# The last expert's second layer with seven block products in place of the plain product, and the stores around it

## The chip, the cores and the metric

The kernel runs on one core of a Trainium2 chip. The metric is the time of one execution on the device in microseconds (us); the runs shown are given by their median. One execution more was taken with the hardware profiler; its trace is what is read here.

## The reference

```python
def _attn_ref(q, k, v):                     # q, k, v: (8, 8, 576, 64)
    k_p = k.reshape(B, H, Sp, 8, D).mean(axis=3)      # keys and values pooled by 8
    v_p = v.reshape(B, H, Sp, 8, D).mean(axis=3)
    scores = scale * np.matmul(q, k_p.transpose(0, 1, 3, 2))
    attn = softmax(scores)
    return np.matmul(attn, v_p)

def _moe_ref(x, domain_probs, w1, w2):      # x: (4608, 512), w1: (4, 512, 1024), w2: (4, 1024, 512)
    p = domain_probs / (domain_probs.sum(-1, keepdims=True) + 1e-09)
    for e in range(E):
        h = np.maximum(x @ w1[e], 0.0)
        out += p[:, e:e + 1] * (h @ w2[e])
    return out
```

The output of the attention, with the heads side by side, is the x of the second part. Four experts each do two layers on all 4608 rows.

## The kernel before

The rows are worked through in nine chunks of 512. Chunks 0 to 7 are the first 512 rows of each batch, chunk 8 holds the remaining 64 of all batches. For each chunk the attention's result lies transposed in `xT`; then the four experts follow. Matmuls are in bf16, sums are kept in f32.

**Block products.** Both layers cut their operands into 2 x 2 blocks and form the product from seven block products in place of eight, with sums of blocks that are made beforehand and afterwards (Winograd's form of Strassen's scheme). For the second layer of expert `e`, `quarters` names the four blocks of the hidden layer H: `a11`, `a12`, `a21`, `a22` (first index: the two row halves of 256 rows, second: the two halves of the 1024 hidden columns). `hidden_sums` makes four sums of them on VectorE: part 0 is S3 = a11 - a21, part 1 is S2 = a22 - S3, part 2 puts a21 + a22 in the place of a21, part 3 puts a12 - S2 in the place of a12. The sums of the weights lie in `wt_bf`, and `w2_bf`'s block b12 is overwritten with b12 - b22. One block product has 2 row blocks of 128 (index `j`) x 4 slices of the hidden columns: 8 matmuls of 128 x 256.

**The order.** Instructions stand in each engine's queue in the order of the program text (a manual schedule). The main loop runs over `g`. At each `g` there are one block product for each of two halves of the first layer (`up_product`, steps 0 to 6, in PSUM banks `units[0]` and `units[1]`, one `g` apart) and one block product of the second layer of the expert before (`down`, steps 0 to 6, in two banks `chains`). `up_product` ends with a copy or a relu on ScalarE (steps 0 to 5 but 4) or a relu with an added part on VectorE (`relu_sum`, steps 4 and 6). `down` ends with two adds into `acc` on VectorE (`add`, line 842: the product by the row's probability plus `acc`); step 4 goes by ScalarE into `addend` and from there by GpSimd into `acc` (lines 775 and 777).

**The end.** With 32 pairs of chunk and expert in `order`, the last `g` is 224. There, the first layer's last product (unit 1, step 6) of chunk 8, expert 3 and step 6 of `down` for expert 2 are issued. Then `down_last` does expert 3's second layer as a plain product: for each of the four output quarters (row half `row`, column half `col`) two row blocks x 8 slices, 64 matmuls in all (line 822), each quarter with two adds. For it, block b12 of the weights, which was overwritten, is loaded again (`load_last_weights`, a DMA on GpSimd's queue). PSUM banks: the two row blocks of a quarter share one, except in the last quarter.

**Stores.** `store` writes a quarter of `acc` to the output. Up to chunk 7 it is one DMA on SP's queue (line 852). For chunk 8 it is two (line 856), one of 64 partitions on SP's queue and one of the other 64 on ScalarE's. In `down_last` three quarters are stored whole (128 KB on each queue), and the last one as two row blocks (64 KB on each queue for each). The kernel's closing stands under line 1122 in the trace: SP waits there for everything that is under way.

Of the kernel before, what the change touches and what calls it, by code (L numbers as in the profile page):

```python
# [9 lines left out]
ACT = mybir.ActivationFunctionType  # L10
ALU = mybir.AluOpType
# [6 lines left out]
def kernel(  # L18
# [10 lines left out]
    nc = tc.nc  # L29

    B, H, S, D = q.shape
    E, DM, F = moe_w1.shape
    P = nc.NUM_PARTITIONS
# [4 lines left out]
    NR = NT // P  # L38
    REM = S - NT
    KC = DM // P  # L40
    FCH = F // P
# [15 lines left out]
    HF, HN, HD, HK = FCH // 2, NT // 2, DM // 2, KC // 2  # L57
    FH = F // 2
    LO, HI = slice(0, HF), slice(HF, FCH)
    BLOCKS = 2  # L60
# [5 lines left out]
    units = [None, None]  # L66
    chains = [psum.tile([P, NT], F32, name=f"o_ps{i}") for i in range(2)]
# [6 lines left out]
    w2_bf = wpool.tile([P, E, FCH, DM], BF16, name="w2_bf")  # L74
    wu_bf = wpool.tile([P, E, 3, HK, FH], BF16, name="wu_bf")
    wt_bf = wpool.tile([P, E, 3, HF, HD], BF16, name="wt_bf")
    acc = const.tile([P, NR, DM], F32, name="acc")
    x_rem = const.tile([P, NPAIR, NT], BF16, name="x_rem")
    ident = const.tile([P, P], BF16, name="ident")
    partial = const.tile([P, 2, 2, NT], F32, name="partial")  # L80
    addend = const.tile([P, BLOCKS, HD], F32, name="addend")
    S2 = const.tile([P, HF, HN], BF16, name="S2")
    S3 = const.tile([P, HF, HN], BF16, name="S3")
# [24 lines left out]
    def choose_rows():  # L108
        nc.vector.memset(begun, 1.0)
        nc.gpsimd.affine_select(  # L110
            out=begun, in_=begun, compare_op=ALU.is_ge, fill=0.0, base=0,
            pattern=[[1, ROWS], [-POOL, SP + 1]], channel_multiplier=ROWS,
        )

    def rows_chosen(half):
        combine(takes[half * PR:(half + 1) * PR], begun[:, :, 0:SP], ALU.subtract, begun[:, :, 1:])
# [104 lines left out]
    p_all = const.tile([P, NBLK, E], F32, name="p_all")  # L221
# [23 lines left out]
    def combine(dst, a, op, b):  # L245
        nc.vector.tensor_tensor(out=dst, in0=a, in1=b, op=op)  # L246
# [352 lines left out]
    hidden = {(0, 0): H_bufs[0], (0, 1): H_bufs[1], (0, 2): H_third, (0, 3): H_bufs[0]}  # L599
    order = [(c, e) for c in range(1, NCH) for e in range(E)]  # L600
# [130 lines left out]
    def quarters(c, e):  # L731
        H_sb = hidden[(c, e)]
        return H_sb[:, 0, 0], H_sb[:, 1, 0], H_sb[:, 0, 1], H_sb[:, 1, 1]

    def hidden_sums(c, e, part):
        a11, a12, a21, a22 = quarters(c, e)
        if part == 0:
            combine(S3[:], a11, ALU.subtract, a21)
        elif part == 1:
            combine(S2[:], a22, ALU.subtract, S3[:])  # L740
        elif part == 2:
            combine(a21, a21, ALU.add, a22)
        else:
            combine(a12, a12, ALU.subtract, S2[:])
# [48 lines left out]
        if fcs.stop == FCH:  # L793
            add(o_ps, c, e, r, slice(0, DM), True)

    room = wu_bf[:, 0, 0].rearrange("p k (i d) -> p (k i) d", d=HD)

    def load_last_weights():

        nc.gpsimd.dma_start(  # L800
            out=room, in_=moe_w2[E - 1][0:FH, HD:DM].rearrange("(fc p) d -> p fc d", p=P)
        )

    def last_weights(fc, col):
        if col and fc < HF:
            return room[:, fc, :]
        return w2_bf[:, E - 1, fc, col * HD:(col + 1) * HD]

    def down_last(c, e):

        H_sb = hidden[(c, e)]
        banks = units[0] + units[1]
        for row in (1, 0):
            for col in range(2):
                cols = slice(col * HD, (col + 1) * HD)
                both = [banks[2 * row + col]] * BLOCKS
                if not row and col:
                    both[1] = chains[0]
                ps = [ps[:, j * HD:(j + 1) * HD] for j, ps in enumerate(both)]
                for j in range(BLOCKS):  # L820
                    for fc in range(FCH):
                        nc.tensor.matmul(  # L822
                            ps[j], lhsT=H_sb[:, fc // HF, row, fc % HF, j * P:(j + 1) * P],
                            rhs=last_weights(fc, col),
                            start=(fc == 0 and (j == 0 or both[1] is not both[0])),
                            stop=(fc == FCH - 1), skip_group_check=True,
                        )
                for j in range(BLOCKS):
                    add(ps[j], c, e, row * BLOCKS + j, cols, False)
                    if not row and col:  # L830
                        store(c, row, cols, j)
                if row or not col:
                    store(c, row, cols)

    def add(o_ps, c, e, r, cols, first):

        prob = p_all[:, c * NR + r, e:e + 1]
        dst = acc[:, r, cols]
        if e == 0 and first:
            nc.scalar.activation(out=dst, in_=o_ps, func=ACT.Copy, scale=prob)  # L840
        else:
            nc.vector.scalar_tensor_tensor(  # L842
                out=dst, in0=o_ps, scalar=prob, in1=dst, op0=ALU.mult, op1=ALU.add,
            )

    def store(c, row, cols, j=None):
        rs = slice(row * BLOCKS, (row + 1) * BLOCKS)
        if j is not None:
            rs = slice(rs.start + j, rs.start + j + 1)
        if c < B:  # L850
            rows = out[c * S:c * S + NT, :].rearrange("(p r) d -> p r d", r=NR)
            nc.sync.dma_start(out=rows[:, rs, cols], in_=acc[:, rs, cols])
        else:
            by_batch = out.rearrange("(b s) d -> s b d", s=S)[NT:S]
            for bb, queue in enumerate((nc.sync, nc.scalar)):
                queue.dma_start(
                    out=by_batch[:, 2 * rs.start + bb:2 * rs.stop:2, cols],
                    in_=acc[bb * REM:(bb + 1) * REM, rs, cols],
                )
# [172 lines left out]
    with tc.manual_schedule(  # L1032
            engines={ENG.PE, ENG.DVE, ENG.Activation, ENG.Pool, ENG.SP}):
        load_q(0)
        load_first(k, "kraw", 0)
        load_first(k, "kraw", 1)
        choose_rows()
        make_identity(nc, ident[:])
        load_first(v, "vraw", 0)
        load_first(v, "vraw", 1)  # L1040
        nc.gpsimd.memset(p_all[:], 0.0)
        load_probs()
        load_w1(0)
        load_w1(1)
        clear()
        rows_chosen(0)
        rows_chosen(1)
        load_w1(2)
        load_w2(0)
        load_w1(3)  # L1050
        attention_first()
        psum_first.__exit__(None, None, None)
        psum_last = ctx.enter_context(
            tc.tile_pool(name="psum_last", bufs=1, space=bass.MemoryType.PSUM))
        units[:] = [[psum_last.tile([P, NT], F32, name=f"unit{u}{i}") for i in range(2)] for u in range(2)]
        load_whole(1, k, "kraw")
        load_q(1)
        load_w2(1)
        load_whole(1, v, "vraw", 2)
        load_w2(2)  # L1060
        first_chunk()


        N = len(order)
        later, amid = pieces_later()
        below_of = [(0, 3)] + order
        sums = {}
        for at, pieces in (((3,), weight_sums(3)[3:]), ((10, 10, 11, 11), weight_sums(1)), ((10, 15, 22, 14), weight_sums(2))):
            for slot, piece in zip(at, pieces, strict=True):
                sums.setdefault(slot, []).append(piece)  # L1070
        POOLED = (4,)
        for g in range(7 * N + 1):
            t, i = divmod(g, 7)
            if i in (0, 2, 3) and 1 < g < 7 * N:
                hidden_sums(*below_of[t], i)
            t2, i2 = divmod(g - 1, 7)
            ups = [(*order[t], 0, i)] if t < N else []
            if 0 <= t2 < N:
                ups.append((*order[t2], 1, i2))

            for args in reversed(ups) if g in amid else ups:
                up_product(*args)
            if g in amid:
                amid[g]()
            if i == 1 and 1 < g < 7 * N:
                hidden_sums(*below_of[t], i)
            if g == 0:

                down_plain(0, 2, NR - 1)
            else:  # L1090
                down(*below_of[t2], i2, t2 % 2, POOLED)
            for piece in later.get(g, ()):
                piece()
            for piece in sums.get(g, ()):
                piece()
            if g == 7 * (N - 2):
                load_last_weights()
        down_last(*order[-1])
# [1 line left out]
_INS = ['q', 'k', 'v', 'moe_domain_probs', 'moe_w1', 'moe_w2']  # L1100
_OUTS = [((4608, 512), 'float32')]
# [25 lines left out]
```

## Time and profile before

| what | us |
|---|---|
| median of 3 runs (lowest, highest) | 489.6 (489.58, 489.82) |
| profiled execution, whole time | 489.93 |
| its span, first to last instruction | 488.2 |
| TensorE busy (share of the span) | 480.5 (98%) |
| VectorE busy | 376.9 (77%) |
| ScalarE busy | 303.8 (62%) |
| GpSimd busy | 119.4 (24%) |
| the plain product of `down_last` on TensorE, 64 matmuls | 476.9 to 483.9 |
| the last add on VectorE | 484.0 to 484.4 |

Times in the profile count from the first instruction. The mean granted clock of TensorE is 0.999. A busy time is the sum of an engine's instructions; instructions on one engine can overlap (a matmul takes 0.27 us from start to end, and the next starts 0.11 us after it), so what an instruction costs its queue is read from start to start.

### The profile page before, as it was taken

To read this page: it belongs to the slowest core of one execution; us is meant where nothing else is said; L and a number is where in the kernel's file an instruction comes from. 1 tells how busy PE (TensorE), PEld (TensorE's weight loads), DVE (VectorE), ACT (ScalarE), POOL (GpSimd) and SP (SyncE) were. 2 spreads that over 40 slices of the span, in tenths; PEclk is the share of its full clock that TensorE was granted. 3 is DMA by queue.
4 is the path that set the end of the run, shared out by engine and by line. 5 is a ranking of instruction groups with operands and counts; after the bars stand their busy time and mean duration, and the time that the engine had idled before them with its cause. 6 is when DMAs were issued, how large, how long until landed. Compare 5 with 4: busy or idle time off the path is not lost.

```text
span 488.2 us, 11522 instructions
## 1 busy us (share of the span) xinstructions
PE 480.5 (98%) x4673; PEld 409.4 (84%) x4678; DVE 376.9 (77%) x758; ACT 303.8 (62%) x576; POOL 119.4 (24%) x120
## 2 busy tenths in 40 slices
PE   8999999999999999999999999999999999999996
PEld 4669568898888888888888888888898888888885
DVE  4779799989768976798679866997678766876674
ACT  5677446855676567656765567556755567556650
POOL 8520504242523154016321442111011101010000
PEclk9999999999999999999999999999999999999999
DMA  9999999994986489345954298311111010004003
GB/s 195 203 209 203 204 170 155 103 90 54 110 110 63 77 86 137 35 83 56 159 50 91 27 165 66 68 23 66 35 23 23 23 64 3 12 23 87 1 1 87
DMA packets 104996, 41.96 MB, mean 86 GB/s; under 512 B 75504, under 2 KB 104432, under 8 KB 104944
## 3 DMA queue, kind: packets, MB, share of 16 engines
q0 software_dynamic: 58496, 22.35, 41.8%
q1 hardware_dynamic: 45328, 17.84, 16.7%
q10 hardware_dynamic: 1120, 1.05, 0.6%
q8 instruction: 36, 0.59, 0.5%
q14 instruction: 16, 0.13, 0.1%
HBM read 45.69 MB, written 9.44 MB: 113 GB/s over the span
## 4 chain that ended last, share of the span: by engine, by line
PE 91%; DMA 3%; ACT 2%; DVE 2%; POOL 1%; issue 1%; POOLq 0%; ACTq 0%
PE unit L695 42%; PE o_ps L763 41%; DMA w_bf<-in_moe_w_dram 3%; PE att L467 1%; PE unit L822 1%; PE o_ps L617 1%; PE att L393 1%; ACT expT L549 1%; PE unit L617 1%; PE unit L393 0%; DVE wt_bf L246 0%; POOL wt_bf L142 0%; ACT qT L378 0%; DVE acc L842 0%; PE work_first L631 0%
## 5 line engine op out<-in xcount | busy, mean ns | idle before, releaser
L842 DVE SCALAR_TENSOR_TENSOR acc<-o_ps,p_all,acc 128x256 f32<-128x256 f32 (+1 forms) x285 | 126.9, 485 | 52.9 <-PE o_ps L763 36.5
L763 PEld LDWEIGHTS <-H 128*128 128x128 bf16 x1320 | 129.1, 98 | 15.5 <-issue 0.6
L695 PEld LDWEIGHTS <-w_bf 128*128 128x128 bf16 x1088 | 105.2, 98 | 13.0 <-issue 0.2
L675 DVE CUSTOM_DVE_ANT_0 H<-unit,partial 128x512 bf16<-128x512 f32 x128 | 87.2, 684 | 23.8 <-ACT partial L710 11.5
L763 PE MATMUL o_ps<-w_bf,H 128*128 128x256 bf16 x792 | 102.6, 273 | 0.4 <-ACT o_ps L771 0.4
L695 PE MATMUL unit<-xT,w_bf 128*128 128x256 bf16 x704 | 100.5, 273 | 0.0
L777 POOL TENSOR_TENSOR acc<-acc,addend 128x512 f32<-128x512 f32 x24 | 30.7, 1279 | 253.2 <-ACT addend L775 202.2
L710 ACT COPY partial<-unit 128x512 f32<-128x512 f32 x128 | 72.3, 592 | 30.2 <-PE unit L695 30.2
L695 PEld LDWEIGHTS <-wu_bf 128*128 128x128 bf16 x816 | 77.6, 98 | 11.7 <-issue 2.5
L695 PE MATMUL unit<-xs,wu_bf 128*128 128x256 bf16 x512 | 77.0, 273 | 0.0
L763 PE MATMUL o_ps<-wt_bf,H 128*128 128x256 bf16 x528 | 68.4, 273 | 0.0
L712 ACT ACTIVATE H<-unit 128x512 bf16<-128x512 f32 x66 | 39.8, 605 | 30.9 <-PE unit L695 30.9
L763 PEld LDWEIGHTS <-S 128*128 128x128 bf16 x528 | 51.7, 98 | 6.0
L716 ACT ACTIVATE H<-unit 128x512 bf16<-128x512 f32 x66 | 39.6, 602 | 25.6 <-PE unit L695 25.3
L708 ACT COPY unit<-unit 128x512 f32<-128x512 f32 x68 | 39.4, 582 | 23.6 <-PE unit L695 18.0
L695 PE MATMUL unit<-xs,w_bf 128*128 128x256 bf16 x256 | 38.4, 273 | 0.0
L840 ACT ACTIVATE acc<-o_ps,p_all 128x256 f32<-128x256 f32 x72 | 30.7, 485 | 9.4 <-PE o_ps L763 7.7
L152 POOL DMA_DIRECT2D kraw<-in_k_dram x20 | 26.3, 1317 | 39.0 <-DMA kraw<-in_k_dram 39.0
L695 PE MATMUL unit<-xT,wu_bf 128*128 128x256 bf16 x240 | 35.7, 272 | 0.0
L763 PE MATMUL o_ps<-w_bf,S 128*128 128x256 bf16 x264 | 34.2, 273 | 0.0
L763 PE MATMUL o_ps<-wt_bf,S 128*128 128x256 bf16 x264 | 34.2, 273 | 0.0
L152 POOL DMA_DIRECT2D vraw<-in_v_dram x20 | 28.4, 1420 | 18.8 <-DMA vraw<-in_v_dram 18.5
(162 smaller groups left out, 500.2 us busy)
## 6 DMA issues: line engine op xcount, KB each, us to landing
out_dram<-acc SPq DMA_DIRECT2D x32, 256.0 KB, 4.2
w_bf<-in_moe_w_dram POOLq DMA_DIRECT2D x10, 512.0 KB, 17.4
q_sb<-in_q_dram POOLq DMA_DIRECT2D x7, 512.0 KB, 9.6
vraw<-in_v_dram POOLq DMA_DIRECT2D x22, 144.0 KB, 6.5
kraw<-in_k_dram POOLq DMA_DIRECT2D x21, 144.0 KB, 5.7
w_bf<-in_moe_w_dram POOLq DMA_DIRECT2D x2, 1024.0 KB, 17.8
w_bf<-in_moe_w_dram POOLq DMA_DIRECT2D x4, 256.0 KB, 7.3
wt_bf<-in_k_dram POOLq DMA_DIRECT2D x4, 144.0 KB, 5.4
```

Source lines behind the costliest of these rows:

```text
L152: nc.gpsimd.dma_start(out=raw[:], in_=rows_of(src, b, 2 * part, 2 * part + 2), accum_op=ALU.add if part else ALU.bypass)
L617: nc.tensor.matmul(out_ps, lhsT=w1_bf[:, e, kc, fc * P:(fc + 1) * P], rhs=xT[:, kc, at], start=(kc == 0), stop=(kc == KC - 1), skip_group_ ...
L675: nc.vector._custom_dve(TENSOR_ADD_SAT, out=dst, in0=ps, in1=part, s0=LARGEST, s1=0.0)
L695: nc.tensor.matmul(ps[:, n * HN:(n + 1) * HN], lhsT=lhs[:, kc, f:f + P], rhs=rhs[:, kc, :], start=(not grows and n == 0 and kc == 0), stop ...
L708: nc.scalar.copy(out=banks[1][:], in_=ps)
L710: nc.scalar.copy(out=part[:, step - 2], in_=ps)
L712: nc.scalar.activation(out=quarter(0, 0), in_=ps, func=ACT.Relu)
L716: nc.scalar.activation(out=quarter(0, 1), in_=ps, func=ACT.Relu)
L763: nc.tensor.matmul(ps[:, j], lhsT=lhs[:, i, j * P:(j + 1) * P], rhs=rhs[:, i, :], start=(not grows and i == 0 and j == 0), stop=(i == HF - 1),
L777: nc.gpsimd.tensor_add(out=dst, in0=dst, in1=addend[:])
L840: nc.scalar.activation(out=dst, in_=o_ps, func=ACT.Copy, scale=prob)
L842: nc.vector.scalar_tensor_tensor(out=dst, in0=o_ps, scalar=prob, in1=dst, op0=ALU.mult, op1=ALU.add,)
```

## The change

`down_last` forms expert 3's second layer from seven block products too. `X` is the pair of banks `units[0]` (one for each row block), `Y` one bank of `units[1]`, `third` the bank of `chains` that step 6 of `down` doesn't use. The order on TensorE: a11 b11 into `X`; step 6 of `down` for expert 2, which is moved behind it and whose result now goes by ScalarE, `addend` and GpSimd into `acc` (`pooled=(6,)`) and no longer by two adds of VectorE; (a21 + a22) with the first weight sum into `third`; S2 with the second weight sum on top of `X`; a12 b21 on top of `Y`, a copy of `X` that ScalarE made after the first product; S3 with (b12 - b22) on top of `X`; (a12 - S2) b22 on top of `third`; a22 with the third weight sum on top of `X`. After the third product ScalarE scales `third` into `spare` (a part of `partial`) and GpSimd adds it to `acc`. After each product from the fourth on VectorE makes two adds. Five of these six results end in `acc` by VectorE, 10 adds in all.

The sums of H are placed thus: part 0 at `g` 223, after the relu of the first layer's step 6 of unit 0 and ahead of step 5's adds of `down`; parts 2 and 1 at `g` 224 ahead of the relu of unit 1's step 6; a12 - S2 goes to `less` (the room of expert 2's a11) behind that relu. `load_last_weights` and its reading side are gone.

All four quarters of chunk 8's last expert are stored whole: eight DMAs in place of ten. In chunks 1 to 7 the quarter of row half 0 and column half 0 is stored by two DMAs, one for each row block, in place of one.

```diff
-    room = wu_bf[:, 0, 0].rearrange("p k (i d) -> p (k i) d", d=HD)
-    def load_last_weights():
-        nc.gpsimd.dma_start(
-            out=room, in_=moe_w2[E - 1][0:FH, HD:DM].rearrange("(fc p) d -> p fc d", p=P)
-        )
-    def last_weights(fc, col):
-        if col and fc < HF:
-            return room[:, fc, :]
-        return w2_bf[:, E - 1, fc, col * HD:(col + 1) * HD]
-    def down_last(c, e):
-        H_sb = hidden[(c, e)]
-        banks = units[0] + units[1]
-        for row in (1, 0):
-            for col in range(2):
-                cols = slice(col * HD, (col + 1) * HD)
-                both = [banks[2 * row + col]] * BLOCKS
-                if not row and col:
-                    both[1] = chains[0]
-                ps = [ps[:, j * HD:(j + 1) * HD] for j, ps in enumerate(both)]
+    def down_last(c, e, flip):
+        w, t = w2_bf[:, e], wt_bf[:, e]
+        a11, a12, a21, a22 = quarters(c, e)
+        less = hidden[(c, e - 1)][:, 0, 0]
+        X = units[0]
+        Y, third = ([bank[:, j * HD:(j + 1) * HD] for j in range(BLOCKS)]
+                    for bank in (units[1][0], chains[1 - flip]))
+        left, right = slice(0, HD), slice(HD, DM)
+        spare = partial[:].rearrange("p u a t -> p (u a t)")[:, 0:BLOCKS * HD].rearrange(
+            "p (j d) -> p j d", j=BLOCKS)
+        def product(banks, lhs, rhs, grows):
+            for j in range(BLOCKS):
+                for i in range(HF):
+                    nc.tensor.matmul(
+                        banks[j][:, 0:HD], lhsT=lhs[:, i, j * P:(j + 1) * P], rhs=rhs[:, i, :],
+                        start=(not grows and i == 0 and (j == 0 or banks is not third)),
+                        stop=(i == HF - 1), skip_group_check=True,
+                    )
+        def add_both(banks, row, cols, room=None, stored=True):
+            if room is not None:
                 for j in range(BLOCKS):
-                    for fc in range(FCH):
-                        nc.tensor.matmul(
...
+                    prob = p_all[:, c * NR + row * BLOCKS + j, e:e + 1]
+                    nc.scalar.activation(out=room[:, j], in_=banks[j][:, 0:HD], func=ACT.Copy, scale=prob)
+                dst = acc[:, row * BLOCKS:(row + 1) * BLOCKS, cols]
+                nc.gpsimd.tensor_add(out=dst, in0=dst, in1=room)
+            else:
                 for j in range(BLOCKS):
-                    add(ps[j], c, e, row * BLOCKS + j, cols, False)
-                    if not row and col:
-                        store(c, row, cols, j)
-                if row or not col:
-                    store(c, row, cols)
+                    add(banks[j][:, 0:HD], c, e, row * BLOCKS + j, cols, False)
+            if stored:
+                store(c, row, cols)
+        product(X, a11, w[:, LO, left], False)
+        combine(less, a12, ALU.subtract, S2[:])
+        for j in range(BLOCKS):
+            nc.scalar.copy(out=Y[j], in_=X[j][:, 0:HD])
+        down(c, e - 1, 6, flip, (6,))
+        product(third, a21, t[:, 0], False)
+        add_both(third, 1, right, spare, stored=False)
+        product(X, S2, t[:, 1], True)
+        add_both(X, 0, right, stored=False)
+        product(Y, a12, w[:, HI, left], True)
+        add_both(Y, 0, left)
+        product(X, S3, w[:, LO, right], True)
+        add_both(X, 1, right)
+        product(third, less, w[:, HI, right], True)
+        add_both(third, 0, right)
+        product(X, a22, t[:, 2], True)
+        add_both(X, 1, left)
 
     def store(c, row, cols, j=None):
...
         if c < B:
             rows = out[c * S:c * S + NT, :].rearrange("(p r) d -> p r d", r=NR)
-            nc.sync.dma_start(out=rows[:, rs, cols], in_=acc[:, rs, cols])
+            parts = [rs]
+            if 0 < c < B and row == 0 and cols.start == 0:
+                parts = [slice(r, r + 1) for r in range(rs.start, rs.stop)]
+            for part in parts:
+                nc.sync.dma_start(out=rows[:, part, cols], in_=acc[:, part, cols])
...
             if i in (0, 2, 3) and 1 < g < 7 * N:
                 hidden_sums(*below_of[t], i)
+            if g == 7 * N:
+                hidden_sums(*order[-1], 2)
+                hidden_sums(*order[-1], 1)
...
                 down_plain(0, 2, NR - 1)
-            else:
+            elif g < 7 * N:
+                if g == 7 * N - 1:
+                    hidden_sums(*order[-1], 0)
                 down(*below_of[t2], i2, t2 % 2, POOLED)
...
-            if g == 7 * (N - 2):
-                load_last_weights()
-        down_last(*order[-1])
+        down_last(*order[-1], (N - 1) % 2)
```

More of the change, by code (lines that the diff above doesn't have):

```diff
@@ L794, in down_plain @@
             add(o_ps, c, e, r, slice(0, DM), True)
-    room = wu_bf[:, 0, 0].rearrange("p k (i d) -> p (k i) d", d=HD)
-    def load_last_weights():
-        nc.gpsimd.dma_start(
-            out=room, in_=moe_w2[E - 1][0:FH, HD:DM].rearrange("(fc p) d -> p fc d", p=P)
-        )
-    def last_weights(fc, col):
-        if col and fc < HF:
-            return room[:, fc, :]
-        return w2_bf[:, E - 1, fc, col * HD:(col + 1) * HD]
-    def down_last(c, e):
-        H_sb = hidden[(c, e)]
-        banks = units[0] + units[1]
-        for row in (1, 0):
-            for col in range(2):
-                cols = slice(col * HD, (col + 1) * HD)
-                both = [banks[2 * row + col]] * BLOCKS
-                if not row and col:
-                    both[1] = chains[0]
-                ps = [ps[:, j * HD:(j + 1) * HD] for j, ps in enumerate(both)]
-                for j in range(BLOCKS):
-                    for fc in range(FCH):
[L822 to L827, printed above, removed]
-                for j in range(BLOCKS):
-                    add(ps[j], c, e, row * BLOCKS + j, cols, False)
-                    if not row and col:
-                        store(c, row, cols, j)
-                if row or not col:
-                    store(c, row, cols)
```

## The prediction

> **What bounds the kernel now.** I read the page first, then the chain of waits in order of time for the end, then the timelines of VectorE, ScalarE and GpSimd there, then the stores. The page: TensorE carries the chain, almost without gaps.
>
> ```profile
> PE 480.5 (98%) x4673; PEld 409.4 (84%) x4678; DVE 376.9 (77%) x758; ACT 303.8 (62%) x576; POOL 119.4 (24%) x120
> ...
> PE 91%; DMA 3%; ACT 2%; DVE 2%; POOL 1%; issue 1%; POOLq 0%; ACTq 0%
> ```
>
> The end of the chain of waits (start, length, what):
>
> ```profile
> 476.06 0.87 PE o_ps L763 x8
> 476.93 6.11 PE unit L822 x56
> 483.05 0.89 PE o_ps L822 x8
> 483.93 0.02 issue
> 483.96 0.48 DVE acc L842
> ```
>
> Eight matmuls take 0.873, one 0.109. The last expert's plain product is 64 of them, without a stall, and VectorE only follows: its last add ends at 484.44. From there to 488.23 it is store and closing. After 70 us TensorE waits once in the whole trace, for 0.4 us (the waits of PE), so a gain before the tail isn't to be had; the tail decides.
>
> VectorE's paces and its state before the tail (start, length, line):
>
> ```profile
> 452.00 0.68 DVE L246 TENSOR_TENSOR S<-H 128x1024 bf16<-128x1024 bf16 x1
> 452.60 0.69 DVE L675 CUSTOM_DVE_ANT_0 H<-unit,partial 128x512 bf16<-128x512 f32 x1
> 453.20 0.68 DVE L246 TENSOR_TENSOR S<-H,S 128x1024 bf16<-128x1024 bf16 x1
> ...
> 475.66 0.88 DVE L842 SCALAR_TENSOR_TENSOR acc<-o_ps,p_all,acc 128x256 f32<-128x256 f32 x2 [0.62 <-PE o_ps L763]
> 476.45 0.68 DVE L675 CUSTOM_DVE_ANT_0 H<-unit,partial 128x512 bf16<-128x512 f32 x1
> ```
>
> Instructions overlap, so starts count: a sum of H or a relu with its sum takes 0.60 from start to start, two adds 0.79 (475.66 to 476.45), the second 0.40 after the first and done 0.48 after its own start. A sum that reads what the instruction just before it wrote takes 0.72 (24.97 to 25.69, weight sums). The two beside it:
>
> ```profile
> 474.79 0.60 ACT L716 ACTIVATE H<-unit 128x512 bf16<-128x512 f32 x1
> ...
> 474.94 1.27 POOL L777 TENSOR_TENSOR acc<-acc,addend 128x512 f32<-128x512 f32 x1 [11.02 <-ACT addend L775]
> ```
>
> **TensorE's part.** 64 matmuls become 56: 8 x 0.109 = 0.87 less, if nothing waits. Expert 2's step 6 only changes places with the first product. From 475.90 on the groups are due 0.873 apart: third product 477.64, S2 product 478.52, a12 product 479.39, S3 product 480.26, (a12-S2) product 481.14, last 482.01. A group's end is 0.16 after the next one's start.
>
> **VectorE's queue.** S3 needs the relu of a21, done at 475.39 (474.79 + 0.60), so it starts at 475.43. Behind it on VectorE wait step 5's adds, ready at 475.66; they free the bank of the third product. Then: S3 0.60, two adds 0.79, a21+a22 0.60, S2 0.60, relu 0.72 (with the dependence of what follows), a12-S2 0.60: free at 479.34. All is there when TensorE asks: a21+a22 ends at 477.50 for 477.64 (the narrowest), S2 at 478.10, a12 at 478.71. The S2 product's adds run 479.34 to 480.13, the a12 product's from its end, 480.47, to 481.26. Two adds are gone: step 6 of expert 2 takes ScalarE and GpSimd now.
>
> **GpSimd's queue.** It gets two adds of 1.27 in a row (before: none in the tail). Step 6 ends at 477.80; two scalings on ScalarE (0.84 for two, L775) and 0.13 to GpSimd, as 474.81 to 474.94 in the trace: 478.81 to 480.08. The third product's scalings are done at 479.57, but its add stands behind the first: 480.18 to 481.45. The S3 product's adds go to the same quarter of `acc` and wait for it, till 481.55 in place of 481.26; and the last product waits for them, since it writes on the banks that they read: 482.10 in place of 482.01. From there VectorE is the chain, at 0.79 a pair: S3's adds 481.56, (a12-S2)'s 482.35, the last 483.14 and 483.54, end at 484.02. Against 484.44 that is -0.42: half of the 0.87 goes to VectorE and GpSimd.
>
> One price is to be added. The sums read two tiles in SBUF, and so does GpSimd's add. The nearest row is a sum of that kind that started 0.04 after GpSimd's add:
>
> ```profile
> 221.54 0.41 DVE L342 TENSOR_TENSOR vp<-vraw 72x512 bf16<-72x512 bf16 x1
> ...
> 221.50 1.58 POOL L777 TENSOR_TENSOR acc<-acc,addend 128x512 f32<-128x512 f32 x1 [11.77 <-ACT addend L775]
> ```
>
> GpSimd took 1.58 in place of the group's median of 1.27, VectorE its usual 0.41 (next start 0.34 later): GpSimd paid 0.32, about what the sum took. Two sums meet GpSimd here: S3 at 475.43 (GpSimd from 474.94 to 476.21) and a12-S2 at 478.74 (from 478.81). Bounds: 0, and VectorE held: S3 till 476.21 (0.78), which with all behind it, a12-S2 till 480.09, brings the end to 484.85, 0.83 later. A gain is excluded, since no work falls away. I take the row's way: S3 costs GpSimd 0.6, which has till 478.81; a12-S2 costs it 0.52, which passes one to one to the end: **484.54, +0.1** against before.
>
> The Trainium skill, "SBUF — State Buffer", section "Who interferes with whom", says that a VectorE instruction with two SBUF inputs contends with a GpSimd instruction that reads SBUF, and that the one that starts second is blocked until the first is through. By it S3, which starts 0.49 into GpSimd's add, is held, and the term is +0.4; the 1.58 agrees that there is contention, and no row here shows VectorE as a clear second.
>
> **The stores.** The last store was 64 KB on each of two queues, SP's at 484.47 (landing 2.27 later) and ScalarE's at 484.75 (2.19 later), landed at 486.93, 2.49 after the last add. Now it is 128 KB each, both issued at once. For the 128 KB pairs the longer landing:
>
> ```profile
> L856 SPq DMA_DIRECT2D out_dram<-acc x1: 597/597/597, 483.1 to 483.1; - x1
> L856 ACTq DMA_DIRECT2D out_dram<-acc x1: 632/632/632, 483.1 to 483.1; - x1
> ...
> DMA to landing us min/median/max: 2.5/2.7/2.8
> ```
>
> Issue 0.03 after the add plus 2.8 (2.85 in the records): 2.88 in place of 2.49, **+0.4**. ScalarE's queue waits for each add, but only stores are left behind it.
>
> The four pairs (481.4, 483.0, 483.8, 484.6) now come 0.8 apart at the end instead of 1.7. Bounds: 0, if a pair is through in less than that (with both queues flowing the slices of the DMA view show up to 378 GB/s, 0.69 for 256 KB), and 1.0 (rival below). The nearest rows are the last three pairs of before (512 KB from 483.12 on), whose landings, 2.2 to 2.8, were not later than alone: **+0.1**.
>
> **The closing and the seven splits.** Stores and transposes count up eight semaphores in turn. In the records the last pair has the second and third of the order in which SP's closing (line 1122) waits: 109 at 486.95, then six more waits, 0.062 each, before its drain at 487.38. Seven more DMAs before the tail and eight instead of ten in it put the last pair on the seventh and eighth: five or six waits are done before the last landing, **-0.3**. The split itself adds seven issues of 0.37 (L852) to SP's queue, each 7 us ahead of the next store there; nothing in TensorE's waits names SP, so 0 (at most 0.4 a chunk if a transposed chunk were due just then). The reload of the weights goes: one issue of 0.84 on GpSimd's queue at 439.5, nothing behind it: 0.
>
> **Sum.** +0.1 + 0.4 + 0.1 - 0.3 = about +0.3. The profiled execution took 489.93, its span 488.23; 1.70 lies around it and stays. So 488.5 and 490.2 there; the median of the runs is 0.33 lower, so **489.9 us**. What a measurement of this kernel can tell from no change is 0.2%, 0.98 us: +0.3 is within.
>
> **The rivals.**
>
> *Stores that queue up (slower).* An isolated pair (479.68) had packets from 481.0 to 482.3: 1.3 us for 256 KB. If each takes that, the three pairs that start to flow at 484.3 end at 488.2, not at 487.2: +1.0, **490.8**. It decides from the point where a pair takes more than its spacing, 0.8. For it: the DMA view shows 8 to 9 tenths busy at about 200 GB/s while one queue flows. Against: 297 to 378 GB/s where two do. The Trainium skill, "SBUF — State Buffer", section "Can I just issue two DMAs to hit both halves?", says no: one DMA on the lower and one on the upper partitions gain 6% together, they serialize. By it this rival would come; the slices with both queues speak against.
>
> *VectorE held by GpSimd's add.* The upper bound above: 484.85 in place of 484.54, **490.2**; past 0.2% only with 0.4 of queueing stores on top.
>
> *TensorE stays the bound (faster).* If adds and GpSimd kept pace, eight groups of 0.873 from 475.90 end at 483.05, the last add at 483.57: -0.87 + 0.4 + 0.1 - 0.3 = -0.7, **488.9**; past 0.2% if 128 KB land as fast as 64. Against: two GpSimd adds alone reach to 481.45.
>
> *The closing does not reorder* (the change doesn't do what it says): +0.3, **490.2**.
>
> **How the numbers follow.** Forecast, with GpSimd's stretch between 0 and 0.6, 0.50 (same 0.47, slower 0.01, faster 0.02); VectorE held 0.20 (same 0.15, slower 0.05); queueing stores 0.15 (slower 0.13, same 0.02); closing not reordered 0.04 (same); TensorE the bound 0.11 (faster 0.07, same 0.04). Together faster 0.09, same 0.72, slower 0.19. The forecast's own range is 489.3 to 490.2; with most of the way to the outer rivals the range is 489.0 to 490.7.
>
> **What would show it.** Right: GpSimd's two adds back to back and the first over 1.27; VectorE's adds of the S3 product released by GpSimd; TensorE waiting before the last product for an add of L842; last add's end between 484.0 and 484.9; SP's closing with its long wait last. S3's start against the end of GpSimd's add settles who pays. Wrong: TensorE without a wait in the tail, landings of the last pair over 3.2, or a difference that arises before 474.

## The result, and the profile after

The changed kernel took 490.79 us in the median (17 runs), the kernel before 489.84 in as many runs beside it; the ratio is 1.0015, with an interval of 1.0008 to 1.0022. By the ratio it is slower by about 0.7 us (0.4 to 1.1; the medians lie 0.95 apart), for the most part inside the 0.2% that was called no change. The forecast was +0.3.

The spans of the two profiled executions, 488.2 and 488.6, give only half of it. They scatter ahead of the tail: the first layer's last block product, to which the two programs differ only by the seven splits and the reload, starts at 475.46 before and at 475.05 after, and in the runs below between 474.8 and 476.0, for one and the same kernel at 475.05 and 475.61. So all that follows counts from the start of that product, **the mark**. The tail repeats: the last add ends 9.23 after the mark in both executions of the changed kernel.

| from the mark | before | after | measured | forecast |
|---|---|---|---|---|
| last add's end | 8.98 | 9.23 | +0.25 | +0.1 |
| from there to the last landing of a store | 2.49 | 3.36 | +0.87 | +0.5 |
| from there to the span's end | 1.30 | 0.99 | -0.31 | -0.3 |
| span's end | 12.77 | 13.58 | +0.81 | +0.3 |

The page after: TensorE still carries the chain. Its 86% in place of 91% says nothing of the tail: the DMA's 8% are input loads (`wt_bf`, `w_bf`) before 55 us, through which the chain runs in this execution.

```profile
PE 479.8 (98%) x4670; PEld 408.5 (84%) x4670; DVE 380.4 (78%) x762; ACT 306.2 (63%) x582; POOL 121.5 (25%) x121
...
PE 86%; DMA 8%; POOL 2%; DVE 2%; issue 1%; ACT 0%; DVEq 0%; POOLq 0%; ACTq 0%
```

The end of the chain of waits was 8 + 56 + 8 matmuls and one add; now it goes through VectorE:

```profile
475.00 0.04 DVE S L246
475.04 1.24 issue
476.27 0.86 DVE acc L855 x2
...
478.97 1.25 DVE H L246
480.23 0.41 DVE acc L855
...
480.68 1.03 PE unit L811 x8
481.71 0.89 PE o_ps L811 x8
482.60 0.02 issue
482.62 1.27 DVE acc L855 x3
```

VectorE's timeline shows why: the two sums that the forecast had at 0.60 to the next start take 1.35 and 1.25.

```profile
475.00 1.35 DVE L246 TENSOR_TENSOR S<-H 128x1024 bf16<-128x1024 bf16 x1 [0.38 <-ACT H L716]
476.27 0.86 DVE L855 SCALAR_TENSOR_TENSOR acc<-o_ps,p_all,acc 128x256 f32<-128x256 f32 x2
477.06 0.68 DVE L246 TENSOR_TENSOR H<-H 128x1024 bf16<-128x1024 bf16 x1
...
478.97 1.25 DVE L246 TENSOR_TENSOR H<-H,S 128x1024 bf16<-128x1024 bf16 x1
480.15 2.43 DVE L855 SCALAR_TENSOR_TENSOR acc<-unit,p_all,acc 128x256 f32<-128x256 f32 x6
```

And GpSimd's timeline shows what they met:

```profile
474.53 1.27 POOL L777 TENSOR_TENSOR acc<-acc,addend 128x512 f32<-128x512 f32 x1 [11.02 <-ACT addend L775]
478.41 1.27 POOL L777 TENSOR_TENSOR acc<-acc,addend 128x512 f32<-128x512 f32 x1 [2.61 <-ACT addend L775]
479.86 1.50 POOL L823 TENSOR_TENSOR acc<-acc,partial 128x512 f32<-128x512 f32 x1 [0.18 <-ACT partial L821]
```

S3 starts at 475.00, 0.47 into GpSimd's add, which ends at 475.80; S3 then ends 0.55 after that. a12-S2 starts at 478.97, 0.56 into the next add, which ends at 479.68; it ends 0.54 after. GpSimd's two adds keep their 1.27. The third one, whose start falls into a12-S2, itself takes longer: 1.50. TensorE pays twice (its timeline): the third product waits 0.40 for a21+a22, and the S3 product starts 1.13 after the one before it in place of 0.87, since it writes on the banks that the S2 product's late adds still read. GpSimd's last add is through at 481.36, before VectorE comes to the S3 product's adds (481.7), so these don't wait for it.

```profile
477.79 1.05 PE L811 MATMUL o_ps<-wt_bf,H 128*128 128x256 bf16 x8 [0.40 <-DVE H L246]
...
479.55 1.04 PE L811 MATMUL unit<-w_bf,H 128*128 128x256 bf16 x8
480.68 1.03 PE L811 MATMUL unit<-w_bf,S 128*128 128x256 bf16 x8
```

The stores (line 873), the last three of them; the last pair is issued at 484.31 on both queues:

```profile
DMA to landing us min/median/max: 3.2/3.3/3.3
```

Before, the later 128 KB pairs had 2.5 to 2.8 here, and the last two DMAs of 64 KB 2.2 to 2.3.

### The profile page after: what moved, and what is told of

It reads as the page before. It is cut to its first block, busy times and chain, and to the rows that moved or that the text cites. A ratio compares the mean times of both kernels' runs of the same rounds, so it can differ in the third digit from the quotient of the medians.

```text
span 488.6 us, 11538 instructions
## 1 busy us (share of the span) xinstructions
PE 479.8 (98%) x4670; PEld 408.5 (84%) x4670; DVE 380.4 (78%) x762; ACT 306.2 (63%) x582; POOL 121.5 (25%) x121
## 3 DMA queue, kind: packets, MB, share of 16 engines
HBM read 45.16 MB, written 9.44 MB: 112 GB/s over the span
## 4 chain that ended last, share of the span: by engine, by line
PE 86%; DMA 8%; POOL 2%; DVE 2%; issue 1%; ACT 0%; DVEq 0%; POOLq 0%; ACTq 0%
PE unit L695 40%; PE o_ps L763 40%; DMA wt_bf<-in_v_dram 5%; DMA w_bf<-in_moe_w_dram 3%; PE o_ps L789 2%; PE att L467 1%; POOL w_bf L207 1%; POOL wt_bf L142 1%; PE att L393 1%; DVE acc L855 1%; PE unit L393 0%; DVE wt_bf L268 0%; DVE H L246 0%; PE att L520 0%; PE att L503 0%
## 5 line engine op out<-in xcount | busy, mean ns | idle before, releaser
L777 POOL TENSOR_TENSOR acc<-acc,addend 128x512 f32<-128x512 f32 x25 | 32.0, 1280 | 256.0 <-ACT addend L775 203.9
L152 POOL DMA_DIRECT2D vraw<-in_v_dram x20 | 29.5, 1474 | 18.1 <-DMA vraw<-in_v_dram 18.1
```

What stands on the lines that cost most here:

```text
L152: nc.gpsimd.dma_start(out=raw[:], in_=rows_of(src, b, 2 * part, 2 * part + 2), accum_op=ALU.add if part else ALU.bypass)
L777: nc.gpsimd.tensor_add(out=dst, in0=dst, in1=addend[:])
```

## The experiments

The theory to be tested had three terms: VectorE and GpSimd cannot both read SBUF for such instructions, and **the one that starts later is held** until the other is through (+0.25 at the last add); the pairs of stores **queue up** (with the 128 KB in place of 64, +0.87 to the landing); and the splits with the whole quarters change **the closing's order** (-0.31). The rivals: VectorE's queue is too long whatever GpSimd does; 128 KB pairs are that slow anyway; the splits do nothing. Runs of which only one execution was taken are read by their traces alone, not by their times.

### Expert 2's step 4 by VectorE

```diff
-                down(*below_of[t2], i2, t2 % 2, POOLED)
+                down(*below_of[t2], i2, t2 % 2, POOLED if t2 < N - 1 else ())
```

> The changed kernel, but expert 2's step 4 in the last chunk goes by two adds of VectorE, so that no GpSimd add runs when S3 starts. Times count from the start of the first layer's last block product (the changed kernel: last add's end 9.23, span's end 13.58). Theory (the later of the two engines is held until the other's instruction is through): S3 takes 0.68 in place of 1.35 and everything behind it on VectorE is 0.67 earlier; a12-S2 then starts at 3.27, ahead of GpSimd's first add (3.36), which is held 0.5 instead, so the GpSimd queue sets the S3 product's adds and the last add ends at 9.1, 0.15 earlier. Rival (VectorE's own queue is too long, GpSimd's adds only happen beside it): S3 still over 1.2, last add's end unchanged at 9.2.

VectorE's and GpSimd's timelines:

```profile
474.87 0.69 DVE L246 TENSOR_TENSOR S<-H 128x1024 bf16<-128x1024 bf16 x1
...
478.19 0.69 DVE L246 TENSOR_TENSOR H<-H,S 128x1024 bf16<-128x1024 bf16 x1
```

```profile
478.28 1.73 POOL L777 TENSOR_TENSOR acc<-acc,addend 128x512 f32<-128x512 f32 x1 [14.90 <-ACT addend L775]
479.97 1.26 POOL L823 TENSOR_TENSOR acc<-acc,partial 128x512 f32<-128x512 f32 x1
```

Further on in VectorE's:

```profile
481.27 0.88 DVE L855 SCALAR_TENSOR_TENSOR acc<-unit,p_all,acc 128x256 f32<-128x256 f32 x2 [0.47 <-POOL acc L823]
```

S3 is back at 0.69. a12-S2 now starts 0.09 ahead of GpSimd's add, and the price changes sides: it keeps its 0.69, and GpSimd takes 1.73, 0.46 more. Here, as in the changed kernel, who starts later pays. The last add ended at 8.79, 0.44 earlier and not 0.15. GpSimd's queue does set the S3 product's adds, as expected: its second add follows the first at once, and its end, 481.23, releases them after VectorE has waited 0.47. Where the other 0.3 of the gain came from is not shown.

### GpSimd's two adds swapped

`down` hands back step 6's GpSimd add, and `down_last` issues it behind that of the third product:

```diff
-        down(c, e - 1, 6, flip, (6,))
+        held = []
+        down(c, e - 1, 6, flip, (6,), held)
         product(third, a21, t[:, 0], False)
         add_both(third, 1, right, spare, stored=False)
+        held[0]()
```

> The changed kernel, but GpSimd's add of expert 2's step 6 is issued behind that of the third product, so that no GpSimd add runs when a12-S2 starts. Theory (the later is held): a12-S2 takes 0.68 in place of 1.25, GpSimd's add of the third product 1.27 in place of 1.50, S3 stays at 1.35; the last add ends 9.0 after the mark, 0.25 earlier. Rival (VectorE's own queue): a12-S2 unchanged, 9.2.

```profile
474.99 1.34 DVE L246 TENSOR_TENSOR S<-H 128x1024 bf16<-128x1024 bf16 x1 [0.37 <-ACT H L716]
...
478.96 0.69 DVE L246 TENSOR_TENSOR H<-H,S 128x1024 bf16<-128x1024 bf16 x1
```

```profile
479.84 1.27 POOL L826 TENSOR_TENSOR acc<-acc,partial 128x512 f32<-128x512 f32 x1 [4.06 <-ACT partial L824]
```

As the theory had it: S3 stays held, a12-S2 is free, GpSimd's add of the third product takes 1.27, the last add ends at 8.98.

### Both apart

> Both together: step 4 on VectorE and GpSimd's two adds swapped, so that neither sum meets a GpSimd add. Theory (the later is held): S3 and a12-S2 0.68 each, GpSimd's adds 1.27 each, TensorE without a wait over 0.1, last add's end at 8.4 after the mark, 0.8 earlier than in the changed kernel and 0.6 earlier than before; time about 0.8 us below the changed kernel, some 0.1 below before (the stores still cost). Rival (VectorE's own queue): 9.2, time as the changed kernel.

VectorE's timeline, the part from S3 to a12-S2, and GpSimd's:

```profile
475.61 0.69 DVE L246 TENSOR_TENSOR S<-H 128x1024 bf16<-128x1024 bf16 x1
...
478.93 0.69 DVE L246 TENSOR_TENSOR H<-H,S 128x1024 bf16<-128x1024 bf16 x1
479.54 0.87 DVE L860 SCALAR_TENSOR_TENSOR acc<-unit,p_all,acc 128x256 f32<-128x256 f32 x2
480.66 1.66 DVE L860 SCALAR_TENSOR_TENSOR acc<-unit,p_all,acc 128x256 f32<-128x256 f32 x4 [0.26 <-PE unit L814]
```

```profile
479.88 1.27 POOL L826 TENSOR_TENSOR acc<-acc,partial 128x512 f32<-128x512 f32 x1 [15.77 <-ACT partial L824]
481.11 1.27 POOL L778 TENSOR_TENSOR acc<-acc,addend 128x512 f32<-128x512 f32 x1
```

The last add ended at 8.41, 0.82 earlier than in the changed kernel and 0.57 earlier than before, and TensorE's waits in the tail are gone. The time was 489.59 us against 489.98 of the kernel before, ratio 0.9988 (0.9978 to 0.9998); that is more than the 0.1 that was expected, and in this trace the last pair landed 2.88 after its issue, as one alone does (see below). VectorE now waits for TensorE (0.26) and not the other way round: of the 0.87 that eight matmuls are worth, 0.57 reach the last add.

### Steps 4 and 6 both by VectorE

As "step 4 by VectorE", and in `down_last`:

```diff
-        down(c, e - 1, 6, flip, (6,))
+        down(c, e - 1, 6, flip, ())
```

> The changed kernel with expert 2's steps 4 and 6 in the last chunk both by VectorE's adds; GpSimd has only the third product's add. Neither sum meets a GpSimd add, as in the kernel with both apart (last add's end 8.41 after the mark), but VectorE has step 6's two adds more (0.79). Theory (after the holds are gone VectorE's queue is the bound, with about 0.5 of waiting for TensorE in it): the last add ends at 8.7, 0.3 later. Rival (TensorE is the bound by then): 8.4.

```profile
479.91 0.87 DVE L855 SCALAR_TENSOR_TENSOR acc<-o_ps,p_all,acc 128x256 f32<-128x256 f32 x2
480.69 2.43 DVE L855 SCALAR_TENSOR_TENSOR acc<-unit,p_all,acc 128x256 f32<-128x256 f32 x6
483.17 0.88 DVE L855 SCALAR_TENSOR_TENSOR acc<-o_ps,p_all,acc 128x256 f32<-128x256 f32 x2
483.96 0.87 DVE L855 SCALAR_TENSOR_TENSOR acc<-unit,p_all,acc 128x256 f32<-128x256 f32 x2
```

8.80 in place of 8.41: the holds are gone here too (S3 and a12-S2 take 0.69 each), and VectorE's adds stand back to back. So VectorE's length is a second price, 0.4 for two adds more, but it comes behind the holds: 0.43 earlier than the changed kernel, although VectorE has four adds more to do.

### The last pair alone

```diff
-            if stored:
+            if stored and (row, cols.start) == (1, 0):
                 store(c, row, cols)
```

> The changed kernel without the stores of three of the four last quarters (those rows are left unwritten); only the last pair is stored, 128 KB on each queue. Theory (pairs queue up behind each other): the pair lands as an undisturbed one did before, 2.6 and 2.85 after its issue in place of 3.18 and 3.33; span's end 13.1 after the mark in place of 13.58. Rival (128 KB pairs need 3.3 as such, or the end of the kernel delays them): 3.2 to 3.3 again, 13.6.

```profile
out_dram<-acc SPq DMA_DIRECT2D x1, 128.0 KB, 2.6
out_dram<-acc ACTq DMA_DIRECT2D x1, 128.0 KB, 2.9
```

Alone, the pair lands 2.60 and 2.88 after its issue, in place of 3.18 and 3.33. The last landing is 2.97 after the last add's end (2.49 before, 3.36 in the changed kernel; the forecast for 128 KB was 2.88). So the 128 KB as such cost about what the forecast said, and 0.4 to 0.45 of the last landing is queueing. This run was executed once; in three executions with the changed kernel's pace (the two of the changed kernel and the one without splits) the later half landed 3.33, 3.41 and 3.17 after its issue. One pair in the kernel before speaks for the rival at first sight: the pair at 479.68, with no other in flight, landed 2.60 and 3.29 after its issue. There, 8 KB of instructions were fetched right behind its last packets, from 482.34 to 482.64; whether its landing waited for them is not tested. The span's end hardly moved, 13.56, which the expectation had missed: with two DMAs in place of eight, the pair counts up the first two of the closing's semaphores, and from its landing to SP's first drain there (the instruction behind the eight waits) it took 0.51 in place of 0.14. The closing's order took back most of what the landing gave.

### Without the seven splits

```diff
-            if 0 < c < B and row == 0 and cols.start == 0:
+            if False:
```

> The changed kernel without the seven split stores. Times count from the start of the first layer's last block product (changed kernel: last add's end 9.23, last landing 12.59, span's end 13.58). Theory (the splits only choose which of the eight completion semaphores the last pair has): SP's half of the last pair moves to the first place of the closing's order and ScalarE's half to the last; six to seven waits of 0.06 follow SP's landing, less the 0.15 by which it lands first: span's end 13.75, last add and landings unchanged. Rival (the splits do nothing): 13.58.

What SP waited for in the closing (us in total, times, longest), before, after, with the last pair alone and without the splits:

```profile
SPq L1122 <- DMA out_dram<-acc: 1.8, 2, 1.1
SPq L1142 <- DMA out_dram<-acc: 2.3, 3, 0.9
SPq L1142 <- DMA out_dram<-acc: 2.2, 1, 2.2
SPq L1142 <- DMA out_dram<-acc: 2.4, 1, 2.4
```

In the last two one long wait comes first, and the others stand behind the landing. The last add stayed at 9.23. From the last landing to SP's first drain in the closing it took 0.36 in place of 0.14; from SP's landing, the first in the order, 0.51. The pairs landed 0.15 earlier in this run, so that the drain itself came only 0.06 later (12.79 after 12.74, less than the 0.17 expected). The span's end, 13.95, is further off, but not by the splits: after SP's last drain there passed 0.78 in place of 0.47, for a reason that the trace doesn't show. That the splits choose the closing's order is shown by the first part: 0.45 before, 0.14 in all eight traces here that have the change's stores and splits, 0.36 and 0.51 in the two without one or the other.

### The plain product with the store part of the change

```diff
-                    if not row and col:
-                        store(c, row, cols, j)
-                if row or not col:
-                    store(c, row, cols)
+                store(c, row, cols)
```

and the seven splits as in the change.

> The kernel before (plain product) with the store part of the change alone: four whole quarters and the seven splits. Times from the same mark (before: last add's end 8.98, last landing 11.48, span's end 12.77). Theory: last add unchanged; the last pair of 128 KB on each queue lands 2.85 after its issue, 1.3 after the pair before it, so 0.4 later than before; the closing has 0.33 less behind it: span's end 12.8 to 12.9. Rival (the store part of the change gains): under 12.6.

Last add 8.98, last landing 2.83 after it, 0.14 from there to the drain, span's end 12.81 against 12.77. The store part alone is worth nothing: 0.34 later landing, 0.31 less closing. With 1.4 to 1.8 between the pairs they did not queue (the last landed 2.50 and 2.80 after its issue), so the queueing comes with the pace at which the seven products hand over their pairs, 0.8 apart, and not from whole quarters as such.

### Stores by rows over all partitions

```diff
-            for bb, queue in enumerate((nc.sync, nc.scalar)):
-                queue.dma_start(
-                    out=by_batch[:, 2 * rs.start + bb:2 * rs.stop:2, cols],
-                    in_=acc[bb * REM:(bb + 1) * REM, rs, cols],
-                )
+            of_row = out.rearrange("(r q s) d -> r q s d", q=2, s=S)
+            for i, queue in enumerate((nc.sync, nc.scalar)):
+                r = rs.start + i
+                queue.dma_start(out=of_row[r, :, NT:S, cols], in_=acc[:, r, cols])
```

> The changed kernel, but each of the last quarters is stored by rows: one DMA of 128 partitions for the first row block on SP's queue after its add, one for the second on ScalarE's. The same eight DMAs and bytes. Theory (a DMA of 64 partitions moves at half rate, and the pairs queue up on that): 2.2 to 2.5 from issue to landing, no queueing, last landing 11.7, span's end 12.7 after the mark, 0.9 earlier than the changed kernel, about as before. Rival (the total rate of the engines is the limit): landings 2.8 to 3.3 again, span's end 13.3 to 13.6.

> Stores by rows, step 4 on VectorE and GpSimd's adds swapped, all in one. Theory: last add's end 8.4, last landing 10.9, span's end 11.9 after the mark, 0.8 to 0.9 us below before. Rival (engines' total rate is the limit): stores now come 0.4 apart and the landing is 3.2 again: span's end 12.4, 0.4 below before.

Both expectations failed, and the question behind them, whether 64 partitions move at half rate, is not answered. The first took 509.49 us (ratio 1.0398, 1.0384 to 1.0412), the second 508.20 (1.0373, 1.0358 to 1.0387). The DMA view of the first, from 484 to 505:

```profile
DMA  1110111111111111111111111111111111111111
GB/s 25 41 43 10 49 47 49 49 49 49 47 49 49 47 49 49 49 49 47 49 49 47 49 49 47 51 47 47 51 47 49 49 47 51 47 49 49 47 49 49
```

The engines are busy at a tenth and move 49 GB/s. Two packets are in flight for 17.4 of the 21 us, where the pair at 479.68 of the kernel before had mostly 13 to 18. The output's side of such a DMA has two batches as its outermost dimension; that this is what sets the two, and not its 128 partitions, no run here tests by itself. The Trainium skill, "DMA: Bandwidth & Descriptors", section "Why a DMA increments its semaphore by 16 and not by 1", says that a DMA is spread over the largest number of engines up to 16 that divides the slowest dimension of both sides, here two; by it two of sixteen would be busy, which agrees with the tenth. The part on VectorE was not touched by it: the last adds ended at 9.23 and 8.41 as in the kernels with other stores.

### Changed kernel and both apart, on one chip

> The changed kernel as it is, on one chip with the next one and the kernel before. Theory: 0.7 to 0.8 us above before; last add's end 9.23 after the mark in this trace too. Rival (the difference is scatter of the runs): within 0.3 us of before.

> The kernel with both apart (step 4 on VectorE, GpSimd's two adds swapped) once more. Theory: 0.4 to 0.6 us below before and 1.1 to 1.3 below the changed kernel; last add's end 8.41, span's end 12.4 to 12.9 after the mark, by how far the last pair queues. Rival (its first interval was luck): within 0.2 us of before.

The changed kernel: 490.89 us against 490.13 of before, ratio 1.0015 (1.0006 to 1.0023), last add 9.23, last landing 3.44 after it. Both apart: 489.75, ratio 0.9994 (0.9985 to 1.0003), last add 8.41, span's end 12.59. So the changed kernel's loss is no scatter, and taking the two engines apart is worth 1.1 us to it. That the result beats the kernel before is likely but not settled: the first interval lies below 1, the second reaches just past it, and 0.3 to 0.4 below falls between the expectation (0.4 to 0.6) and the rival (0.2). Between the two traces of this kernel the last pair landed 2.88 and 3.11 after its issue, with the same spacing of 0.8 to 0.9: in the first it did not queue at all by the measure of the pair alone. How far the pairs queue varies from run to run.

## Why the prediction was right or wrong

The forecast, +0.3 us and no change that can be told, was right in sign, and in kind by less than it had counted on; measured were +0.7 by the runs and +0.8 by the trace. Around the kernel before at 489.6 its range of 489.0 to 490.7 is -0.6 to +1.1, and +0.7 lies in it, but above the +0.6 to which the forecast's own case reached. The last add (+0.15) and the landing (+0.37) both cost more than forecast; that the sum stayed under 0.2% is in part luck. Of the prediction's signs of being right, the last add's end came (9.23, between 8.54 and 9.44), and the closing waits for the last pair near its end. Three did not come in the changed kernel: GpSimd's two adds are 0.18 apart and the first takes 1.27, the S3 product's adds are not released by GpSimd, and TensorE does not wait before the last product but before the third and the S3 product. One of its signs of being wrong came: a half of the last pair landed 3.33 after its issue. By its steps:

- **TensorE, and the order in which the engines meet: right where nothing is held.** With both apart every product starts where it was forecast (the third 2.18 after the mark, the last 6.55), and the last add ends at 8.41; the working's 484.02, for GpSimd's adds not swapped and before any price, is 8.56. The path that it saw at the end, GpSimd's second add releasing the S3 product's adds and these delaying the last product, is that of the run with step 4 by VectorE (a wait of 0.47, the last product at 6.89 in place of 6.55). In the changed kernel S3's hold put the third product at 2.74 and a12-S2 0.64 later than forecast, and with that came another path, through a12-S2 and the S2 product's adds.
- **VectorE's paces: right.** 0.60, 0.79 and 0.71 (for 0.72) stand in the trace after, and with both apart the queue is free of a12-S2 at 3.88, as counted (479.34 less 475.46).
- **Who pays when a sum meets GpSimd's add: the step that failed.** The prediction took GpSimd, by the row at 221.54, and so 484.54: a price of 0.52 on the last add. VectorE paid, for S3 (1.35) and for a12-S2 (1.25), and the two meetings cost 0.82 (9.23 against 8.41 with both apart). The row was misread. Its sum started 0.04 after GpSimd's recorded start and was not held, and it is so in all thirteen traces (GpSimd's add takes 1.58 or 1.59). In each case in which GpSimd paid (1.58, 1.73, 1.50) its add ended 1.13 after the sum; a whole add takes 1.27, so, as an estimate, an add is in the sum's way only from some 0.14 after its recorded start. By that the sum at 221.54 was the first of the two, and S3, 0.47 after GpSimd's start, the second. The row could not show what happens to a sum that clearly comes second. The rival "VectorE held by GpSimd's add" is what happened; it put the last add's end at 484.85, 9.39 after the mark; 9.23 came, mainly because the hold ends some 0.1 before the recorded end of GpSimd's add: S3 cost the queue 0.67 more (1.27 to the next start in place of 0.60) and not 0.78.
- **The stores: right in mechanism, short in size.** For the 128 KB, 2.88 after the add was forecast, and the pair alone landed at 2.97. The term for queueing was 0.1 and measured 0.4 to 0.5. The rival "Stores that queue up" came about half way: its +1.0 was 0.4 to 0.5. The prediction's reason, that the last three pairs of before landed as if alone, does not hold in its own rows: they are 0.7 apart on SP's queue, but two of the three have 64 KB on each queue, half the bytes, and of these ScalarE's first DMA, issued at 483.79 behind the 128 KB, landed 2.75 after its issue, where the last one took 2.19.
- **The closing: right.** -0.31 for -0.3, shown by the runs without the splits and without the other stores.
- **The seven splits and the reload cost nothing that shows**, as stated: TensorE's waits after 70 us are those of the tail alone.

The Trainium skill's rule on the shared port ("SBUF — State Buffer", "Who interferes with whom": the later of the two is blocked) agrees with every one of these runs: 1.35, 1.25 where VectorE came later, 1.73, 1.50 where GpSimd did, 0.69 and 1.27 where they were apart; only the recorded start can't be taken for the moment that decides, as the row at 221.54 shows. By it the forecast would have been 490.2. The Trainium skill's rule in the same page that two DMAs on the two partition halves serialize ("Can I just issue two DMAs to hit both halves?") is borne out in part: in a pair alone the second queue's packets begin when the first's are nearly through (before, 481.0 to 481.9 and 481.7 to 482.3), but pairs 0.8 apart queued by only 0.5, where 1.0 was worked out for full serialization.

## What to carry to other kernels

A sum that VectorE makes of two SBUF tiles and an add that GpSimd makes in SBUF are to be placed as if they shared one engine: moving a sum to another time, for the sake of TensorE, moves it into other neighbours, and here two such meetings cost 0.82 at the last add, nearly what 8 matmuls were worth (0.87). Judge a change of the tail from a mark just ahead of it: spans scattered by a microsecond, the tail by hundredths. And a store that comes earlier need not land earlier by as much, nor does a kernel end with its last landing: the pairs before it (0 to 0.5) and the order in which the closing waits (0.3) together weigh as much as was to be gained at the last add (0.57).

## What the runs showed of the hardware that was not expected

A bf16 sum of 128x1024 on VectorE (0.68) took 1.35 when it started 0.47 into a GpSimd add in SBUF, and that add took 1.73 in place of 1.27 when the sum started 0.09 ahead of it. A shorter sum that started 0.04 after the add's recorded start was not held, and the add took 1.58, in all thirteen traces. A DMA of 128 KB whose output side has an outermost dimension of 2 moved with its like at 49 GB/s in all, where the same bytes as 64 partitions by two rows moved at 145 to 214 GB/s with one queue flowing and up to 378 with both (the kernel before, slices of 0.16 us). The kernel's closing waits for its eight DMA semaphores one after the other, 0.06 each, so that it matters by 0.3 us which of them the last store counts up.
